# Down weights fetched a block ahead, TensorE in written order and a layer norm in pairs, in a fused forward and backward kernel

## Chip, cores, metric

One core of a Trainium2 chip. The metric is device time in microseconds (us) of one execution; a profile of one execution of each kernel is read beside it. Lower is better. A verdict of faster or slower needs 2%.

## The reference, cut to what matters

The function adds three terms and returns its value with the gradients of nine inputs:

```python
xn = _layernorm(x, axis=-1)                              # x: 2048 x 1024, bf16
return x + conv_branch(xn, k, v, shift_k, ssm_k, ssm_D) + mlp(xn, W_gate, W_up, W_down)

def mlp(x, W_gate, W_up, W_down):                        # 1024 -> 3584 -> 1024
    gate = x @ W_gate;  up = x @ W_up
    gate = gate * (gate > 0)
    return (gate * up) @ W_down
# conv_branch: short shift convolution of k, times v, a long convolution (FFT), times xn
```

The kernel computes the MLP and its gradients with 8064 products of 128x128 by 128x512. The convolution branch, eight groups of 128 channels, is interleaved with them.

## The kernel before

Rows are cut into 16 tiles of 128, hidden columns into 7 blocks of 512. The first phase, `hidden`, runs 14 times (two halves of the rows by 7 columns; I call each a block, 0 to 13). In a block, for pairs of row tiles: a gate product, an up product and a down product (`ps_g`, `ps_u`, `ps_h`; each 8 matrix instructions, 1.73 us). `wg`, `wu` and `wdT` are the block's weights, each of four pieces of 256 KB. A slot set is room for one such weight; there are four, three in use and one spare. A tile of the normalised rows is flipped (transposed) on TensorE (`pst_x`), and VectorE copies it to `xnT`, which the gate and up products read; `goT`, the transposed gradient of the output, comes by DMA transposes.

```python
LN_CHUNKS = (1, 1, 1, 1, 2, 2, 4, 4)        # tiles of the layer norm that are handled together

def gemm8(self, ps, xT, w):
    for kt in range(self.DT):
        self.pri.pin(self.nc.tensor.matmul(ps[:], ...))     # pin: only once the branch runs

# hidden(), one block; sp counts pairs of row tiles
def load_gate(): nw[0] = self.col_block(Wg, nb, "wg", spare)      # at the block's start
def load_up():   nw[1] = self.col_block(Wu, nb, "wu", su)         # after its last up product
def load_down(): nw[2] = self.row_block_T(Wd, nb, "wdT", sg)      # after its last gate product:
                                                                  # four DMA transposes
...
w, sets, spare = tuple(nw), (spare, su, sg), sd
```

All these transfers are issued from one engine, SyncE, in a fixed order: a transfer that waits for something holds up all behind it. The branch runs on a clock of its own: each product counts 1.73 us of "product time", and a step of the branch is written between two products when that clock has passed its turn.

```python
A_START = 55_000                 # ns of product time: the branch's first inputs are asked for
SLOT = 1780                      # ns between steps of the branch, 72 to a group
def steps(self):
    self.shift_rows()            # a small table: TensorE, ScalarE (sk_t), stored to sk_d
    nx = self.loads_1(0)         # hn, gt, xt (xt reads xn_d, the normalised rows), sD
    self.loads_2(nx)             # kp, vt, skb
    yield 16000                  # then the groups begin
    ...
```

## Time and profile before

| | kernel before |
|---|---|
| median of the runs beside the changed kernel | 1953.41 us (1952.6 to 1957.48, 4 runs) |
| span of the profiled run | 1950.2 us |
| first gate product of block 1 | 67.28 us |
| first product after `hidden` (`ps_d`) | 704.07 us |
| TensorE waits for `wu`, `xnT`, `Y` | 10.3, 8.4, 3.2 us |

The two instants cut the span in three: the start, where the layer norm feeds TensorE; blocks 1 to 13; the rest. The prediction below shows the views and how they are read.

### The profile page before, as it was taken

How to read it: one execution, taken by the hardware profiler on the slowest of the kernel's cores; microseconds unless marked ns; L12 is line 12 of the kernel's file. 1: busy time of each engine (PE TensorE's matmuls, PEld its weight loads, DVE VectorE, ACT ScalarE, POOL GpSimd, SP SyncE). 2: the span in 40 equal slices, each digit the busy share in tenths (PEclk: the TensorE clock that was granted, in tenths of full speed). 3: DMA queues.
4: the chain of work that ended last, by engine and by line, in shares of the span. 5: the costliest groups of instructions: out<-in, count | busy, mean ns of one | idle time of the engine just before them, and what ended most of it. 6: DMA issues, size and time to landing. Idle time of an engine off the chain costs nothing.

```text
span 1950.2 us, 35936 instructions
## 1 busy us (share of the span) xinstructions
PE 1896.9 (97%) x15295; PEld 882.9 (45%) x15526; DVE 908.1 (47%) x1358; ACT 628.6 (32%) x861; POOL 15.5 (1%) x38
## 2 busy tenths in 40 slices
PE   8999899999999999999999999999999999999998
PEld 3444444444444444444444444444444444444443
DVE  5777677777676673443443443510222222222222
ACT  5664354354445344344345345321000000000000
POOL 1100000000000000000000000000000000000000
PEclk9999999999999999999999999999999999999999
DMA  9985676974774884464744543376999854554551
GB/s 253 242 193 143 164 185 165 220 195 131 178 179 131 199 231 129 112 175 126 204 128 134 141 125 106 106 192 214 234 254 248 206 132 122 122 121 122 121 124 35
DMA packets 615985, 319.08 MB, mean 164 GB/s; under 512 B 450952, under 2 KB 585104, under 8 KB 615824
## 3 DMA queue, kind: packets, MB, share of 16 engines
q1 hardware_dynamic: 605328, 295.79, 61.4%
q10 hardware_dynamic: 9216, 16.78, 2.8%
q0 software_dynamic: 1280, 4.20, 0.6%
q8 instruction: 121, 1.98, 0.4%
q14 instruction: 40, 0.33, 0.1%
HBM read 141.56 MB, written 95.44 MB: 122 GB/s over the span
## 4 chain that ended last, share of the span: by engine, by line
PE 65%; issue 2%; DMA 0%; DVE 0%; ACT 0%; SPq 0%
PE ps_w L1006 19%; PE ps_x L1188 19%; PE ps_o L1154 10%; PE ps_d L1006 8%; PE ps L72 4%; PE ps_d L1019 1%; PE ps_h L795 1%; PE ps_u L795 1%; PE ps_g L795 1%; PE ps_w L1019 0%; DMA wu<-in_B_W_up_dram 0%; DMA xn_nat<-xn_d 0%; PE pst L304 0%; ACT K L76 0%; DVE flp L315 0%
## 5 line engine op out<-in xcount | busy, mean ns | idle before, releaser
L1006 PE MATMUL ps_w<-ugs,xn_nat 128*128 128x512 bf16 x1674 | 377.1, 379 | 5.0 <-issue 3.2
L795 PEld LDWEIGHTS <-xnT 128*128 128x128 bf16 x1792 | 170.9, 98 | 230.5 <-issue 20.6
L1006 PEld LDWEIGHTS <-xn_nat 128*128 128x128 bf16 x1728 | 165.0, 98 | 199.4 <-issue 5.5
L795 PE MATMUL ps_u<-wu,xnT 128*128 128x512 bf16 x865 | 205.7, 382 | 12.9 <-DMA wu<-in_B_W_up_dram 10.3
L795 PE MATMUL ps_g<-wg,xnT 128*128 128x512 bf16 x864 | 206.3, 384 | 10.9 <-DVE xnT L824 8.4
L795 PE MATMUL ps_h<-wdT,goT 128*128 128x512 bf16 x872 | 202.4, 379 | 2.6 <-issue 1.4
L1201 ACT ACTIVATE w<-xn,m 128x512 f32<-128x512 bf16 x32 | 24.3, 806 | 559.5 <-issue 317.2
L1188 PE MATMUL ps_x<-wgT,ggT 128*128 128x512 bf16 x879 | 197.6, 379 | 0.9
L1188 PE MATMUL ps_x<-wuT,guT 128*128 128x512 bf16 x877 | 197.3, 379 | 0.9
L1154 PE MATMUL ps_o<-wd,hT 128*128 128x512 bf16 x878 | 192.6, 379 | 0.9
L1006 PE MATMUL ps_d<-g_nat,hs 128*128 128x512 bf16 x740 | 167.5, 379 | 3.1 <-issue 2.4
L1154 PEld LDWEIGHTS <-hT 128*128 128x128 bf16 x896 | 87.7, 98 | 105.7
L1188 PEld LDWEIGHTS <-ggT 128*128 128x128 bf16 x896 | 87.7, 98 | 105.7
L1188 PEld LDWEIGHTS <-guT 128*128 128x128 bf16 x896 | 87.7, 98 | 105.7
L899 DVE SCALAR_TENSOR_TENSOR ru<-ru,ps_u 128x512 bf16<-128x512 bf16 x112 | 76.7, 685 | 125.6 <-issue 53.3
L315 DVE STREAM_TRANSPOSE flp<-C 128x1024 f32<-128x1024 f32 x48 | 90.5, 1931 | 93.7 <-ACT C L76 93.7
L795 PEld LDWEIGHTS <-goT 128*128 128x128 bf16 x896 | 85.6, 98 | 104.0 <-issue 4.3
L1190 DVE CUSTOM_DVE_ANT_0 gx<-ps_x,gy 128x512 f32<-128x512 f32 x32 | 22.1, 691 | 216.6 <-PE ps_x L1188 202.5
L76 ACT CAST C<-ps 128x1024 bf16<-128x1024 f32 x96 | 92.5, 1015 | 91.8 <-PE ps L72 91.2
L926 ACT CAST gh<-ps_h 128x512 bf16<-128x512 f32 x112 | 65.3, 584 | 160.2 <-PE ps_h L795 143.5
L315 DVE STREAM_TRANSPOSE flp<-B 128x1024 f32<-128x1024 f32 x48 | 90.6, 1938 | 49.5 <-ACT B L76 49.5
L76 ACT CAST B<-ps 128x1024 bf16<-128x1024 f32 x96 | 94.1, 1016 | 58.8 <-PE ps L72 54.2
(169 smaller groups left out, 1484.1 us busy)
## 6 DMA issues: line engine op xcount, KB each, us to landing
ug_d<-ru SPq DMA_DIRECT2D x112, 256.0 KB, 4.9
ugs<-ug_d SPq DMA_DIRECT2D x112, 256.0 KB, 4.8
wg<-in_B_W_gate_dram SPq DMA_DIRECT2D x56, 256.0 KB, 4.8
wu<-in_B_W_up_dram SPq DMA_DIRECT2D x56, 256.0 KB, 4.9
h_d<-ht SPq DMA_DIRECT2D x112, 128.0 KB, 2.2
hs<-h_d SPq DMA_DIRECT2D x56, 256.0 KB, 4.7
out_dram<-wi SPq DMA_DIRECT2D x56, 256.0 KB, 2.2
gt<-in_grad_out_dram SPq DMA_DIRECT2D x32, 256.0 KB, 5.3
```

The lines of the kernel that those rows point to most:

```text
L72: self.pri.pin(self.nc.tensor.matmul(out, lhsT=lhsT, rhs=rhs, start=start, stop=stop))
L76: self.pri.pin(self.nc.scalar.copy(out=out, in_=in_))
L315: self.pri.pin(self.nc.vector.transpose(out=df[:, c0:c0 + 32, :], in_=sf[:, c0:c0 + 32, :]))
L795: self.pri.pin(self.nc.tensor.matmul(ps[:], lhsT=xT[:, kt * P:(kt + 1) * P], rhs=w(kt), start=(kt == 0), stop=(kt == self.DT - 1)))
L899: self.pri.pin(nc.vector.scalar_tensor_tensor(out=ru[s][:, 1, :], in0=ru[s][:, 0, :], scalar=0.0, in1=ps[:], op0=ALU.is_gt, op1=ALU.mult))
L926: self.pri.pin(nc.scalar.copy(out=gh[:], in_=ps[:]))
L1006: self.pri.pin(self.nc.tensor.matmul(ps[:], lhsT=lhsT(st), rhs=rhs(st), start=(st == 0), stop=(st == self.ST - 1)))
L1019: self.pri.pin(self.nc.tensor.matmul(ps[i][:], lhsT=lhsT(i, st), rhs=rhs(i, st), start=(st == 0), stop=(st == self.ST - 1)))
L1154: nc.tensor.matmul(ps[:], lhsT=hT[:, kt, :], rhs=self.wd[:, kt, oc], start=(kt == 0), stop=(kt == self.FT - 1))
L1188: nc.tensor.matmul(ps[:], lhsT=T[:, kt, :], rhs=W[:, kt, oc], start=(i == 0), stop=(i == n - 1))
L1190: V.tensor_tensor_reduce(out=gx[:, oc], in0=ps[:], in1=gy[:, oc], scale=1.0, scalar=0.0, op0=ALU.add, op1=ALU.add, accum_out=m[:, ob:ob + 1])
L1201: nc.scalar.activation(out=w[:, oc], in_=xn[:, oc], func=ACT.Identity, scale=m[:, 5:6], bias=m[:, 4:5])
```

## The change

Its intent: take the waits away in which TensorE stands for `wu`, for flipped tiles `xnT` and for the branch's product `Y`. Cut to its core:

```diff
-    LN_CHUNKS = (1, 1, 1, 1, 2, 2, 4, 4)
+    LN_CHUNKS = (1, 1, 1, 1, 2, 2, 2, 2, 2, 2)
@@ gemm8, flip_xn, warm: TensorE in written order from the start
-            self.pri.pin(self.nc.tensor.matmul(...))
+            self.pri.pin(self.nc.tensor.matmul(...), always=True)
+            if mid is not None and kt == 3:
+                mid()                                # a flip in the middle of an up product
@@ weights of the next block
-                    nw[0] = self.col_block(Wg, nb, "wg", spare)
+                    nw[0] = self.col_block(Wg, nb, "wg", sg)
-                    nw[2] = self.row_block_T(Wd, nb, "wdT", sg)
+                    nw[2].append(self.row_piece_T(Wd, nb, "wdT", spare, q))
@@ gate_up: wg after the last gate product, wu after the last up product
+                if end:
+                    load_gate()
...
                 if not ahead:
-                    if sp == 0:
-                        load_gate()
                     yield from gate_up(sp)
+                    load_down(sp // 2)
-            w, sets, spare = tuple(nw), (spare, su, sg), sd
+            w, sets, spare = tuple(nw), (sg, su, spare), sd
@@ block 0, first two pairs: gate, flip, up, gate, up (with a flip in it) instead of
@@ flip, gate, flip, gate, up, up; the norm's last two pairs and the branch's tables in block 1
+                if n == 1 and sp < 4:
+                    chunk()
+                    if sp == 2: ... tables()
@@ the branch
-    SLOT = 1780
+    SLOT = 1760
-        yield 16000
+        yield 11000
-A_START = 55_000
+A_START = 66_000
@@ slots(): one step of the complex product before the two flips instead of after
+        yield None, qy
         flg = self.flip(...)
         yield None, flg
         yield None, flg
-        yield None, qy
```

## The prediction

> **What bounds the kernel now.** I read the page's busy times first.
> ```profile
> span 1950.2 us, 35936 instructions
> ...
> PE 1896.9 (97%) x15295; PEld 882.9 (45%) x15526; DVE 908.1 (47%) x1358; ACT 628.6 (32%) x861; POOL 15.5 (1%) x38
> ```
> TensorE is busy for 1896.9 of 1950.2 us, and the change neither adds nor removes one of its products. It can only win the 53.3 us in which TensorE is idle, and time in which it runs at a lower clock. The timeline fixes 7.9 us of the idle time at the end (last product over at 1942.3) and 1.5 us before the first dummy product; the change touches neither. What is left is in the waits of TensorE, by instruction and releaser (total, times, longest):
> ```profile
> PE ps_u L795 <- DMA wu<-in_B_W_up_dram: 10.3, 9, 4.5
> PE ps_g L795 <- DVE xnT L824: 8.4, 6, 3.6
> PE ps L72 <- DVE Y L80: 3.2, 3, 1.7
> ```
> The third row is the convolution branch, the first two the MLP's first phase (`hidden`, until about 705 us). The next view is TensorE in order of time over the first 75 us (start, length, idle time before it in brackets):
> ```profile
> 18.64 0.61 PE L822 MATMUL pst_x<-ident,ln_x 128*128 128x128 bf16 x8
> 21.45 3.58 PE L795 MATMUL ps_g<-wg,xnT 128*128 128x512 bf16 x8 [2.21 <-DVE xnT L824]
> ...
> 40.20 3.62 PE L795 MATMUL ps_u<-wu,xnT 128*128 128x512 bf16 x16
> ...
> 51.77 5.31 PE L795 MATMUL ps_g<-wg,xnT 128*128 128x512 bf16 x16 [3.60 <-DVE xnT L824]
> ```
> Sixteen products take 3.62 us, but 5.31 after a wait of 3.60 us; eight take 1.90 elsewhere and 3.58 after 2.21 us of waiting. A long wait thus costs 1.7 us more in clock. Why the wait at 51.77 is so long is in VectorE and ScalarE around it:
> ```profile
> 48.42 0.17 DVE L746 TENSOR_SCALAR ln_b<-ln_s 128x4 bf16<-128x4 f32 x1 [3.35 <-ACT ln_j L732]
> ...
> 50.42 0.69 DVE L927 TENSOR_TENSOR ru<-ru,gh 128x1024 bf16<-128x1024 bf16 x1
> 51.02 1.29 DVE L824 COPY xnT<-pst_x 128x1024 bf16<-128x1024 bf16 x2
> ```
> TensorE had flipped tiles 6 and 7 by 46.4, but their copies stand in VectorE's queue behind the layer norm of four later tiles, whose four row sums ScalarE finishes at 48.4. Last, the queue of transfers around the longest wait for `wu`, and TensorE there:
> ```profile
> 201.16 5.31 SPq L803 DMA_TRANSPOSE wdT<-in_B_W_down_dram  x4
> 206.56 2.74 SPq L88 DMA_DIRECT2D kp<-in_A_k_dram  x4
> ...
> 213.92 1.97 SPq L788 DMA_DIRECT2D wu<-in_B_W_up_dram  x4
> ```
> ```profile
> 211.68 1.90 PE L795 MATMUL ps_g<-wg,xnT 128*128 128x512 bf16 x7
> 218.13 3.59 PE L795 MATMUL ps_u<-wu,xnT 128*128 128x512 bf16 x8 [4.55 <-DMA wu<-in_B_W_up_dram]
> ```
> `wu` has one slot set, so it can be asked for only when the last up product of a block is over. Four transposes of `wdT` and the branch's next inputs (6.7 us of issuing) stand in the queue before it. In blocks without the branch's inputs the same waits are 0.7 to 1.5 us, ended by the transposes alone.
>
> **What the Trainium skill says.** "TensorE: Matmul & The Clock Gate", Part 1: The HAM clock gate: after an idle window of about 3.4 us the array runs at half rate until about 3.4 us of activity have passed. Half of 3.4 is 1.7, and the three dips here (at 21.45, 51.77, 218.13) cost 1.68, 1.69 and 1.69 us; the first came after only 2.21 us of idling, so the limit isn't sharp here. The same page, Architectural detail: VectorE and ScalarE are strict first-in-first-out; the copies at 51.02 agree. "DMA: Bandwidth & Descriptors", Anatomy of one DMA: a DMA's semaphore wait happens on the issuing sequencer. This agrees: the queue waited 142 us in all (100 to 800 us) for `ht`, with later loads behind it. "Advanced Engine Details and Errata", X-Bar Transpose (TRN2): transposes are as fast as plain transfers. The landing agrees (median 3.4 us against 4.9 for `wu`); but a transpose holds the issuing queue for a median of 1.25 us, a piece of `wu` for 0.42.
>
> **The change, part by part.**
>
> 1. *Order of the weights.* The four transposes leave the place ahead of `wu`: one goes after each pair of rows, into the set that the block before freed. In exchange `wg` loses its second set and is asked for after the block's last gate product. Until its use come two up and two down products, 4 x 1.73 = 6.9 us and up to 2 us of branch work. Four pieces take 2.0 to 2.5 us to issue and land 4.9 us after issue; TensorE eats a piece each 0.43 us. So the first piece has about 2 us in hand and the last about 0.5 (an estimate). `wu` has the same 6.9 us, now with a free queue: in three block changes where the transposes happened to be over early (wu issued at 455.98, 505.74, about 604) it waited for nothing. Gain: 10.3 + 1.7 of clock = 12.0, less 1 left over: 11 us.
>
> 2. *The branch's start and pace.* 55 to 66, then 16 to 11, with 2 after both: the branch's groups start at 79 instead of 73 us of product time. A group is 72 slots, so the eight end at 79 + 576 x 1.76 = 1092.8 instead of 1098.3: nothing for the end. But I placed the loads of `kp`, `vt`, `skb` (slot 50 of a group) in the blocks of 24 x 1.73 = 41.5 us. Before: 73 + 50 x 1.78 = 162.0, that is 37.4 us into a block, between the last gate product (34.6) and the last up product (38.1): the 4.55 us wait. The next is at 41.0. After: 167.0, 0.9 into a block, then 3.1, 5.2, 7.4; none falls into 34.6 to 41.5, where `wg` and `wu` are now asked for. I take this into the 11.
>
> 3. *One half-step of the complex product ahead of the two flips.* At 483.26 the last `Y` step ran behind two flips of 1.9 us, and TensorE began at 483.97. It now goes before them: 2.7 of 3.2 us.
>
> 4. *The first products.* Between the first gate product (10.31) and the end of the gate pair 6, 7 (57.0) lie 18 products of 1.73 and eight flips of 0.55 us: 35.5 of 46.7 us. So 11 us can be lost at most. Traced order makes gate 0, flip 1, up 0, gate 1, half of up 1, flip 2, the rest: each copy (0.69 us) now lies beside at least 0.9 us of products. That takes out 0.8 + 2.2 + 0.8 of waits and 1.7 of clock. Pairs shorten what stands before the copies of tiles 6 and 7 from four row sums (4.4 us) to two (2.3), and from four subtractions (1.68) to two (0.88): about 3 of the 3.6 us and the clock's 1.7. But the norm's own chain sets a floor: tile 2 was normalised at 16.8, 3 at 20.1, 6 and 7 at 39.8, and the fixed order would want them at 17.0, 20.2 and 39.4; I give 1 to 3 us back. Gain: 3.8 + 1.7 + 3 + 1.7 = 10.2, less 2.2: 8 us.
>
> Against it: the branch's first inputs (15 us of issuing, from 83.5 in the profile) now begin 24.5 us into block 1 and so may stand before its `wg` at 34.6; the tables also come a quarter-block later. I put 2.5 us on this.
>
> Sum: 11 + 2.7 + 8 - 2.5 = 19.2; 1952.85 - 19.2 = 1933.7, so **1934 us**, 1.0% less.
>
> **Rivals.** *`wg` takes `wu`'s place as the wait.* For it: one slot set, 0.5 us in hand for the last piece, and stores in the queue ahead. Against: the three block changes without a wait. 13 changes at 0.7 us would eat 9: 1943. *The fixed order stalls TensorE at the start*, as no other product may pass a late tile. For it: the norm's times in 4. Against: at 18 to 27 the scheduler's own order waited as well. The start would give nothing: 1942. *VectorE becomes the bound of the branch with the slot at 1.76.* Against: it is busy for 32 to 39 of each 50 us there; worth a few us at most. *Everything comes off*: all 12 + 3.2 + 11 would be 1926.5.
>
> **Range and chances.** 1925 to 1944: the two first rivals at one end, all gains and a few small issue gaps at the other. Faster by over 2% would need 1913.8, that is 39 us; the idle time that can be had (53.3 - 9.4 - about 5 of dummy and first tile) with 5 of clock comes to 44, of which the change addresses 26. 2%. Slower by over 2%: 1%.
>
> **What would show it.** Right: waits for `wu` under 2 us in all; none for `Y` above 0.5; no wait of over 2 us before a gate product in the first 60 us; block 1's first gate product near 59 instead of 67.28; the same busy time of TensorE after the start. Wrong: a row of waits of gate products for `wg`, above all near 100 us; `pst_x` waiting for `ln_x`; or the saved time coming back as waits of the branch on VectorE.

## The result, and the profile after

The changed kernel took 1940.03 us (median; 1939.31 to 1943.27, 4 runs, none over 1.5% above the fastest), the kernel before 1953.41 beside it. A ratio is the mean time of one kernel's fast runs over the mean of the other's in the same rounds, so not quite the ratio of the medians; here it is 0.9931, 95% interval 0.9913 to 0.9948: 0.7% less. Predicted: 1934, 1925 to 1944. The measured gain, 13.4 us, is 70% of the predicted 19.2.

The page after, to be held against the first two lines that the prediction shows:

```profile
span 1938.3 us, 35924 instructions
...
PE 1891.5 (98%) x15294; PEld 881.5 (45%) x15526; DVE 910.2 (47%) x1378; ACT 630.3 (33%) x863; POOL 15.3 (1%) x38
```

The span is 11.9 us shorter, with TensorE's instructions unchanged. The waits of TensorE after (total, times, longest):

```profile
PE ps_g L795 <- DMA wg<-in_B_W_gate_dram: 9.3, 3, 7.3
PE ps_g L795 <- DVE xnT L827: 3.9, 3, 2.9
...
PE pst_x L824 <- DVE ln_x L776: 1.8, 2, 1.6
...
PE ps L72 <- DVE flp L315: 1.5, 3, 0.8
```

The 10.3 us for `wu` and the 3.2 for `Y` are gone. In their place gate products wait 9.3 us for `wg`, 7.3 of it at once. The waits for `xnT` have halved, and a flip (`pst_x`) waits for a normalised tile.

TensorE in the first 62 us, as in the prediction's third fence:

```profile
22.18 0.62 PE L824 MATMUL pst_x<-ident,ln_x 128*128 128x128 bf16 x8 [1.63 <-DVE ln_x L776]
...
27.39 1.90 PE L795 MATMUL ps_g<-wg,xnT 128*128 128x512 bf16 x8 [2.87 <-DVE xnT L827]
...
47.70 3.63 PE L795 MATMUL ps_g<-wg,xnT 128*128 128x512 bf16 x16 [0.20 <-DVE xnT L827]
...
61.52 3.62 PE L795 MATMUL ps_g<-wg,xnT 128*128 128x512 bf16 x16
```

The gate pair of tiles 6 and 7 begins at 47.70 instead of 51.77, after 0.20 us of waiting instead of 3.60, and takes 3.63 instead of 5.31. But tile 3's flip (22.18) and the gate product behind it (27.39) wait 4.5 us.

The 7.3 us wait, on TensorE:

```profile
106.07 0.59 PE L72 MATMUL ps<-hT,RH 128*128 128x512 bf16 x2
113.96 3.59 PE L795 MATMUL ps_g<-wg,xnT 128*128 128x512 bf16 x8 [7.30 <-DMA wg<-in_B_W_gate_dram]
```

This is the first gate product of block 2; at 3.59 instead of 1.90 us it pays the clock's 1.7 too. What stood in the transfer queue before `wg` (start, time of issuing, transfer):

```profile
88.97 0.34 SPq L96 DMA_DIRECT2D sk_d<-sk_t  x1
...
90.31 1.42 SPq L88 DMA_DIRECT2D gt<-in_grad_out_dram  x2
98.12 1.31 SPq L88 DMA_DIRECT2D xt<-xn_d  x2
...
106.24 1.58 SPq L88 DMA_DIRECT2D skb<-sk_d  x1
...
109.74 2.22 SPq L788 DMA_DIRECT2D wg<-in_B_W_gate_dram  x4
```

And what the queue itself waited for between 80 and 112 us:

```profile
SPq L88 <- DMA xn_d<-ln_x: 6.1, 2, 5.6
SPq L96 <- ACT sk_t L76: 4.6, 1, 4.6
```

The slots of `wg` were free from about 96 us (the last gate product of block 1). It was asked for at 109.74, behind all of the branch's first inputs. In these, `xt` waited for the last normalised rows, which the norm in pairs delivers from block 1 (last store issued at 91.94; before, from 72.14).

By thirds of the span: block 1 begins 5.8 us earlier (67.28 to 61.52), the blocks 1 to 13 take 5.0 us less (636.8 to 631.8), the rest 1.1 us less. At both instants the branch stands at the same step, so the thirds can be compared.

### The profile page after: what moved, and what is told of

It is laid out like the page before. It is cut to its first block, busy times and chain, and to the rows that moved or that the text cites. A ratio compares the mean times of both kernels' runs of the same rounds, so it can differ in the third digit from the quotient of the medians.

```text
span 1938.3 us, 35924 instructions
## 1 busy us (share of the span) xinstructions
PE 1891.5 (98%) x15294; PEld 881.5 (45%) x15526; DVE 910.2 (47%) x1378; ACT 630.3 (33%) x863; POOL 15.3 (1%) x38
## 4 chain that ended last, share of the span: by engine, by line
PE 66%; issue 2%; DMA 0%; DVE 0%; ACT 0%
PE ps_w L1032 19%; PE ps_x L1214 19%; PE ps_o L1180 10%; PE ps_d L1032 8%; PE ps L72 4%; PE ps_h L795 1%; PE ps_u L795 1%; PE ps_d L1045 1%; PE ps_g L795 1%; PE ps_w L1045 1%; DMA ugs<-ug_d 0%; PE pst L304 0%; DMA xn_nat<-xn_d 0%; DVE flp L315 0%; DVE o L1230 0%
## 5 line engine op out<-in xcount | busy, mean ns | idle before, releaser
L1130 ACT CAST wi<-ps_w 128x512 bf16<-128x512 f32 x108 | 63.7, 590 | 154.7 <-PE ps_w L1032 150.0
```

What stands on the lines that cost most here:

```text
L1130: self.pri.pin(nc.scalar.copy(out=wo[0][:, d, :], in_=ps[:]))
```

## The experiments

My theory after the result: the 7.3 us come from the transfer queue, which stands at `xt` until the norm's last rows are stored. Rivals: the volume of the branch's inputs, wherever they stand; and the one slot set of `wg`, which can only be refilled after the last gate product. At the start, I took the two waits left for queue order on ScalarE and VectorE, against the norm's own chain as the floor.

### 1. `xt` behind the other first inputs

```diff
-        self.load_time(xt, self.xn_d, cg)          # third of the first inputs
+        if gi: self.load_time(xt, self.xn_d, cg)
...
         self.loads_2(nx)
+        self.load_time(nx["xt"], ...)              # first group: last
```

> Changed kernel, but for the first group the two loads of xt (which read xn_d) go behind the other first inputs of the branch instead of third. Queue theory (the transfer queue stands at xt from 91.7 to 98.1 us waiting for the last stores of xn_d, and everything behind it, wg of block 2 included, is late by that): the other inputs fill the 6.4 us, wg is asked for 6 to 7 us earlier, its 7.3 us wait falls to 0 to 2 us and the 1.7 us of clock goes too; 1932 us (1930 to 1935). Volume theory (the branch's inputs take the DMA engines, so wg lands late wherever it stands): as many bytes in the same stretch, the wait stays at 5 us or more; 1938 to 1941. One-set theory (wg can only be asked for after the last gate product, that alone is the wait): stays at 7; 1940.

Measured: 1938.4 us, ratio 0.9926 (0.9912 to 0.9941). The queue no longer waits for `xn_d`, but `wg` is asked for at 108.44 instead of 109.74 and TensorE still waits 5.23 us for it there. The issuing of the inputs, from 89.35 to 104.7, has merely lost its gap, and part of the gap was filled by slower issuing (the four pieces of `kp` took 5.04 us instead of 3.60, a store behind the inputs 2.14 instead of 0.36):

```profile
112.27 2.68 PE L797 MATMUL ps_g<-wg,xnT 128*128 128x512 bf16 x6 [5.23 <-DMA wg<-in_B_W_gate_dram]
```

So the wait for `xt` is 2.1 of the 7.3 us. My queue theory in its first form falls; volume and one-set both stand.

### 2. The branch 14 us later

```diff
-A_START = 66_000
+A_START = 80_000
```

> Changed kernel with the branch started 14 us later (80 instead of 66 us of product time), so that its first inputs are asked for after wg and wu of block 2. Queue and volume theory: no wait of gate products for wg at the second block change, 9 us less; but the third group's first inputs then come 30.5 us into block 11 and may cost 1 to 2 us: 1932 (1930 to 1936). One-set theory: the wait stays, 1940. If later placing costs the branch's end anything, TensorE would show waits after 1290 us; I expect none.

Measured: 1931.56 us, ratio 0.9898 (0.9879 to 0.9918). No product waits for `wg` anywhere. The queue:

```profile
94.45 2.13 SPq L788 DMA_DIRECT2D wg<-in_B_W_gate_dram  x4
...
105.36 0.55 SPq L96 DMA_DIRECT2D sk_d<-sk_t  x1
```

`wg` goes out as soon as its slots are free, and the branch's inputs follow behind `wu`. `wg` still has one slot set, and at all 13 block changes nothing waits for it: the one-set theory falls. What counts is that the branch's inputs do not stand between the last gate product and the next block. This run cannot tell the queue from the volume, as both foresaw it. The landing times can: the one that the trace of the changed kernel has for `wg` at this change is 4.6 us after issue, against a median of 4.3 for all of its `wg`. So `wg` was issued late and did not land late; volume can have acted only by slower issuing. In time, the intervals of this run and of the changed kernel still touch (0.9879 to 0.9918, 0.9913 to 0.9948), so it is the waits that show the cause. The 2.0 us of waits for `wg` at the change from block 6 to 7 are gone as well, which I had not expected. The branch pays with one wait of 2.58 us for a flip of its own, at 136 us.

### 3. The norm's last two pairs in block 0 again

```diff
-                if n == 1 and sp < 4:
+                if ahead:
                     chunk()
-                    if sp == 2: ... tables()
+                    if sp == 6: ... tables()
```

> Changed kernel with the last two pairs of the layer norm traced in block 0 again instead of block 1 (pairs kept), the tables right after. Queue theory: the last xn_d store is issued near 75 instead of 92 us, xt waits for nothing, the first inputs are all asked for by 98 and wg 8 us earlier; its wait falls from 7.3 to 0 to 1.5: 1931 to 1934, unless the norm's row sums in block 0 hold back down products there (up to 3 us more: then 1936). Volume theory: wait of 5 or more, 1938 to 1941.

Measured: 1943.27 us, ratio 0.9952 (0.9937 to 0.9967): a miss. `xt` now waits for nothing, yet the wait for `wg` is 8.23 us. The tables, traced earlier, go through ScalarE ahead of the copy `sk_t`; its store, which stands in front of the branch's inputs, is issued at 94.74 instead of 88.97 (the queue waited 4.3 us for `sk_t`), all inputs follow later, and `wg` goes out at 112.70. The earlier norm alone does not help: there is more than one thing for the block of inputs to wait for.

### 4. The norm's chunks of four again

```diff
-    LN_CHUNKS = (1, 1, 1, 1, 2, 2, 2, 2, 2, 2)
+    LN_CHUNKS = (1, 1, 1, 1, 2, 2, 4, 4)
```

> Changed kernel with the old chunks of the layer norm (two of four tiles at the end instead of four pairs). If pairs are what took the 3.6 us wait for the copies of tiles 6 and 7 away: it comes back with 2 to 4 us and possibly the clock's 1.7, block 1's first gate product at 64 to 66 instead of 61.5. Queue theory: the last xn_d store moves from 92 to near 80, so the wait for wg at the second block change falls to 0 to 3 us. Net 1934 to 1940. If pairs gave nothing at the start, 1932.

Measured: 1943.28 us, ratio 0.9954 (0.9934 to 0.9975). The gate pair of tiles 6 and 7 waits 2.19 us again and takes 5.32 us; block 1 begins at 66.42 instead of 61.52. Of these 4.9 us, 1.6 are a clock dip after gate 3 that has nothing to do with the chunks (see 5), so pairs are worth about 3.3 us here: 2.0 of wait and 1.7 of clock before tile 6, less 0.4 of small differences. That takes the dip off in full; if without it the wait for the copies had been longer instead, pairs are worth up to 4.9. The wait for `wg` at the second block change is 4.41 us, a miss against 0 to 3: the queue's wait for `xn_d` is gone altogether (last store issued at 71.25, `xt` at 96.07, 0.3 us after `gt`), and over 4 us stay, as in experiment 1.

### 5. Without the fixed order of TensorE

```diff
-        if self.strict or always:
+        if self.strict:
```

> Changed kernel without the fixed TensorE order before the branch begins (gate, up and down products, flips and dummies again ordered by the scheduler); trace order, pairs and weights unchanged. If the fixed order is what won the start (waits before gate products 8.4 to 3.9 us): block 1's first gate product moves from 61.5 back to 64 to 67 us, total 1942 to 1946. If the order in which the products are written, or the pairs, did it: 61 to 62.5, total 1939 to 1942. The wait for wg at the second block change stays at 5 to 9 us either way.

Measured: 1941.3 us, ratio 0.9954 (0.9934 to 0.9973). The two builds turned out to have the same instructions in the same order on all five engines: with the products written in this order, the scheduler would have kept it. So this part of the change does nothing, and this run is a repeat of the changed kernel. As such it shows two things. The ratio of one program differs by 0.2% (0.9931, 0.9954). And gate 3, after the same wait (2.87 and 2.86 us), took 1.90 us in one profile and 3.43 in the other, so whether a wait of this length costs the clock's 1.7 us differs from run to run:

```profile
27.75 3.43 PE L795 MATMUL ps_g<-wg,xnT 128*128 128x512 bf16 x8 [2.86 <-DVE xnT L827]
```

Block 1 began at 64.12 instead of 61.52.

### 6. The norm of tiles 4 and 5 later

```diff
                 yield from first_gate_up(0)
-                chunk()
-                yield from first_gate_up(2)
+                yield from first_gate_up(2, chunk)     # chunk after tile 3's flip
```

> Changed kernel with the layer norm of tiles 4 and 5 traced after the flip of tile 3 instead of before gate 2. My reading of the two waits left at the start (1.63 us of the flip, 2.87 us of gate 3): tile 3's square root stands behind two row sums of tiles 4 and 5 on ScalarE, its copy behind their norm on VectorE. Then both fall, together from 4.5 to 1 us or less, but tiles 4 and 5 then stand behind the norm of 6 and 7, whose input lands only at 31 us: 1 to 4 us of new waits before gates 4 and 5. Block 1's first gate product at 59 to 61.5; total 1937 to 1940. If instead the norm's own chain is the floor, both waits stay and nothing moves: 61.5, 1940.

Measured: 1941.91 us, ratio 0.9957 (0.994 to 0.9974); experiment 5, in the same rounds, is the control with 0.9954. Tile 3's flip now waits 0.79 us instead of 1.63, and gate 3 not at all: it ends at 25.4 instead of 29.3. So those waits were queue order, not the norm's own chain. But the flip of tile 4 waits 5.7 us:

```profile
34.55 1.89 PE L824 MATMUL pst_x<-ident,ln_x 128*128 128x128 bf16 x16 [5.70 <-DVE ln_x L776]
```

ScalarE shows why (the norm's next row sum, of tile 6, holds the queue until its input lands; the square root of tiles 4 and 5 is behind it):

```profile
31.54 1.06 ACT L732 ACTIVATE ln_j<-ln_x 128x1024 bf16<-128x1024 bf16 x1 [4.61 <-DMA ln_x<-in_A_q_dram]
```

I had named this wait, at 1 to 4 us. Block 1 begins at 64.39, a miss against 59 to 61.5.

### 7. The same, with the input of tiles 6 and 7 asked for earlier

```diff
+    load(5)
     goT = [b.load_T(g, i, "goT", 8 + i) for i in range(4)]
-    load(5)
```

> As the run before, and the input of tiles 6 and 7 asked for ahead of the four transposes of goT (its landing near 24 instead of 31 us). Same reading: the new waits before gates 4 and 5 go too; block 1's first gate product at 57 to 58.5, total 1935 to 1937 with the wait for wg at the second block change still there (7 us, perhaps longer by what TensorE arrives earlier: then up to 1939). If the wait for wg absorbs all of the gain, the total is 1940 although block 1 begins earlier.

Measured: 1943.33 us, ratio 0.9963 (0.9947 to 0.9979). The wait before tile 4 falls to 0.98 us. The next one of its kind appears: a down product waits 3.91 us for `ru` (46.04), behind the norm of tiles 8 and 9, whose input is still late. Block 1 begins at 63.26, a miss against 57 to 58.5. In the chain of the norm, each wait removed so far has uncovered the next; experiment 11 asks for more of the inputs earlier.

### 8. Kernel before, with the weights alone

```diff
-                    nw[0] = self.col_block(Wg, nb, "wg", spare)   # at the block's start
+                    nw[0] = self.col_block(Wg, nb, "wg", sg)      # after the last gate product
-                    nw[2] = self.row_block_T(Wd, nb, "wdT", sg)
+                    nw[2].append(self.row_piece_T(Wd, nb, "wdT", spare, q))   # one per pair
```

> Kernel before with only the new order of the weights (wg asked for after the last gate product, then wu; wdT a piece per pair into the freed set). If the transposes ahead of wu were the cause of its waits: the 0.7 to 1.5 us waits at five block changes go (about 5 us), total 1944 to 1948; at the change where the branch's inputs stand in the queue (4.55 us and 1.7 us of clock) a wait of wu of 1 to 5 us stays, since those are still asked for there. If wg takes their place: waits of gate products for wg of over 5 us in total and 1950 or more.

Measured: 1945.12 us, ratio 0.9971 (0.9954 to 0.9988), as expected. Of the nine waits for `wu` one is left, 3.11 us at the change where the branch's inputs stand in the queue; no product waits for `wg`. From block 1 to the end of `hidden` the profile is 5.3 us shorter. It also has two waits that I had not named and did not follow up: 3.3 us for `goT` in block 0, and 1.5 us of an up product for ScalarE's copy `gh` in block 1.

### 9. Kernel before, with the complex-product step alone

The edit is the last hunk of the change.

> Kernel before with only the branch's complex-product step moved ahead of the two flips. If that order made the three waits of TensorE for Y (3.2 us): they fall to 0.5 us or less, total 2.5 to 3.2 us under the kernel before, about 1948 to 1950. If the flips, now later by a slot, are waited for instead: the waits for flp grow from 0.8 to 3 us and the time stays.

Measured: 1949.88 us, ratio 0.9991 (0.9971 to 1.001). The waits for `Y` are gone (3.2 to 0), those for flips unchanged (0.8). The time does not tell it from nothing: the gain is as small as the repeat error of experiment 5, and the longest wait for `wu` happened to be 5.24 instead of 4.55 us. Shown in the waits, not in the time.

### 10. Kernel before, with the branch's start and pace alone

```diff
-        yield 16000
+        yield 11000
-A_START = 55_000
+A_START = 66_000
-    SLOT = 1780
+    SLOT = 1760
```

> Kernel before with only the branch's start (66 and 11 instead of 55 and 16) and pace (1760 instead of 1780). Placement theory (a load of the MLP's weights waits if the branch's inputs stand ahead of it in the queue): the 4.55 us wait for wu at the fourth block change goes (inputs now 0.9 us into a block), and a new wait for wu of 3 to 8 us comes at the second block change, where the first inputs now stand ahead of wdT and wu; total 1949 to 1955. If the waits for wu have nothing to do with the branch's inputs: the 4.55 us wait stays and none comes.

Measured: 1958.8 us, ratio 1.0037 (1.0015 to 1.0059): slower by 7 us, 4 more than I allowed. The 4.55 us wait is gone, and the new one is where the placement theory puts it, at the second block change:

```profile
120.26 1.44 PE L795 MATMUL ps_u<-wu,xnT 128*128 128x512 bf16 x3 [6.21 <-DMA wu<-in_B_W_up_dram]
```

In this kernel the norm is in its old chunks and `wg` has its second slot set. So neither of them is needed for a wait at this change: the place of the branch's first inputs in block 1 brings one there too. It is not quite the same wait, as here `wu` is the one held up, and four transposes (5.8 us of issuing) still stand between the inputs and it.

### 11. The branch later, the norm later, its inputs earlier

Experiments 2 and 6 together, and `load(5)`, `load(6)` ahead of the transposes of `goT`, `load(7)` right behind them.

> Changed kernel with the branch started at 80, the norm of tiles 4 and 5 traced after the flip of tile 3, and the inputs of the norm's pairs 5, 6 and 7 (tiles 6 to 11) asked for ahead of or between the transposes of goT. If what is left at the start is only that each pair of the norm stands at the head of VectorE's and ScalarE's queues until its input lands behind the transposes: no wait over 1.2 us in the first 70 us, block 1's first gate product at 57 to 58.5, and no wait for wg: total 1924 to 1928. If the order of the norm itself is the floor: a wait of 2 to 4 us appears before a down product or a flip again and the total is 1928 to 1932. If asking early delays goT or wdT: waits of down products for goT.

Measured: 1932.04 us, ratio 0.9903 (0.9888 to 0.9918), no better than experiment 2. The start is as hoped: tiles 6 and 7 begin at 44.58 (46.78 in experiment 2). Then `wg` (2.5 us), `wu` (1.1) and `goT` (1.5) are waited for. In block 0 the transfer queue is never empty: `wg` could have gone out at about 48 and went at 54.62, behind four transposes of `wdT` and one of `goT`.

### 12. The same, with block 1's `wdT` behind `wg` and `wu`

```diff
-                        if sp == 0:
-                            for q in range(4): load_down(q)
                 if ahead and sp + 4 < HS:
                     yield from gate_up(sp + 4)
+                    if sp == 2: ...
+                        for q in range(4): load_down(q)
```

> As the combined run before (branch started at 80, norm of tiles 4 and 5 later, inputs of the norm earlier), but block 1's four pieces of wdT are asked for after wg and wu instead of in the middle of block 0. That run gained the start (gate pair 6, 7 at 44.6 us against 46.8 with the later start alone) and lost it again in waits for wg and wu (3.6 us) and goT (1.5), which I put down to the transfer queue being full with transposes until 54.6 us. If so: wg is asked for near 49 and waits for nothing, at most 1 us of waiting for wdT before block 1's first down product; total 1926 to 1929. If what holds wg back is the volume of block 0's transfers rather than their order: wg or wdT waits for 2 to 4 us as before; 1931 to 1933.

Measured: 1928.87 us (1927.45 to 1929.68), ratio 0.9886 (0.9865 to 0.9907), the fastest of all, 1.1% under the kernel before. `wg` goes out at 47.92 and costs 0.5 us of waiting, `wdT` none. Block 1 begins here:

```profile
58.12 3.62 PE L795 MATMUL ps_g<-wg,xnT 128*128 128x512 bf16 x16
```

Its interval lies below that of the changed kernel (0.9913 to 0.9948), though from other rounds; it overlaps that of experiment 2, so the later start is the certain part and the better start of about 2.5 us rests on the profile.

## Why the prediction was right, and where it was not

Time, range and class held, and most steps did. Some of the size is luck: by the repeat in experiment 5 (0.9954) the gain is about 9 us, not 13. Of the signs of being wrong that the prediction named, two came: gate products wait for `wg` (one long wait from 106.6 us, where a row of waits was named, and two short ones later), and `pst_x` waits for `ln_x`; and of the signs of being right, "no wait of over 2 us before a gate product in the first 60 us" failed (2.87). The terms, as the prediction has them:

| step | predicted | measured | from |
|---|---|---|---|
| 1. weights | 11 | 10.0 | waits for `wu` 10.3 and clock 1.7 gone; 2.0 of new waits for `wg` at the change from block 6 to 7 |
| 3. complex product | 2.7 | 2.5 | waits for `Y` 3.2 gone, for flips 0.7 more |
| 4. start | 8 | 5.8 | block 1 at 61.52 instead of 67.28 |
| "Against it" | -2.5 | -9.0 | wait for `wg` 7.3 and clock 1.7 |
| sum | 19.2 | 9.3 | |
| time | 19.2 | 13.4 (medians), 11.9 (profiles) | |

2.6 us of the profile's gain are in no row: 1.1 lie after `hidden`, the others are spread over small gaps, and 0.2% is the repeat error.

- **Step 1 held**, mechanism and size: the waits for `wu` go with the new order of the weights alone (experiment 8, whose edit moves `wdT` and `wg` together). The rival that `wg` takes the place of `wu` because of its one slot set is refuted by experiments 2 and 8, in which no product waits for `wg`. The two small waits for `wg` in the change from block 6 to 7 are the 0.5 us in hand, overdrawn: two transposes of `goT` stood before it.
- **Step 2 held in both halves.** The placement of the later inputs, worked out from 72 slots and blocks of 41.5 us, took away the 4.55 us wait (experiment 10). It was not carried to the first inputs as strictly.
- **The step that failed is the term "Against it"**: "the branch's first inputs ... may stand before its `wg` at 34.6; ... I put 2.5 us on this." The wait came at that place for that reason (experiments 2 and 10), but measured 7.3 us and 1.7 of clock. The term was too small even by the prediction's own numbers: inputs from 24.5 us into the block, 15 us long, end at 39.5, 4.9 us behind the place of `wg`, which had about 2 us in hand; with the clock's 1.7 that is some 4.6 us (an estimate), and I put 2.5. Beyond that I left out that the inputs can wait themselves: for the table `sk_t` (4.6 us) and for the norm's last rows (6.1 us), which the pairs had moved into block 1. `wg` went out 13.6 us behind its place (61.52 + 34.6 = 96.1): the 4.9 us, 3.0 because the store of `sk_d` began 27.45 us into the block, 3.9 because the inputs took 18.9 us from there to the last one, and 1.9 for two stores behind them. Taking away the wait for the norm's rows alone leaves 5.23 us of waiting (experiment 1) or 4.41 (experiment 4); no run takes away the wait for `sk_t` alone, so its share is argued, not shown.
- **Step 4 was too high by 2.2 us.** Its order part was put at 3.3 us (5.5 less 2.2 for the norm's floor) and came to 0.6 up to the first down product (31.47 to 30.86), although that stretch's clock dip of 1.7 us had gone: tile 3's copy came to stand behind the norm of tiles 4 and 5 as tiles 6 and 7's had before. Its pairs part was put at 4.7 (3, and 1.7 of clock) and is about 5.2 between the two single profiles, 3.3 to 4.9 by experiment 4. The fixed order is no part of it (experiment 5). How much of the clock's 1.7 us a run has differs from run to run, and so the 5.8 itself is uncertain by a us or two: with the old start, block 1 begins at 65.61 to 68.32 in four profiles (kernel before, experiments 8, 9 and 10), with the new one at 60.60 to 64.12 in four (changed kernel, experiments 1, 2 and 5).
- **Two slips in the prediction's sums** change nothing in it. Seven flips, not eight, lie between 10.31 and 57.0, which makes 35.0 of 46.7 us and 11.7 that can be lost; and all gains together give 1926.65, not 1926.5.

What stays open: why experiment 2 also loses the waits at the change from block 6 to 7, and how the 2.5 us of experiment 12 over experiment 2 look in time with more runs. For the first, the queue gives a hint: in the changed kernel two stores of the branch's `gv` come shortly before (345.62), the two transposes of `goT` begin 0.2 us after the last gate product and take 4.31 us; in experiment 2 no such store stands there, and they begin 1.3 us before that product is over and take 2.67.

## What to carry to other kernels

When several streams of work share one in-order transfer queue, draw up for each weight load the stretch between the freeing of its slots and its use, and keep every other batch of loads, the first one above all, out of it; count a batch with the waits of its own members, not with its issuing alone. Work that you delay to smooth one place (the norm in pairs) may be what such a batch waits for. And compare two builds' instruction order before timing them: a "fixed order" may be the order you already had.

## What the Trainium skill lacked or had wrong

- "TensorE: Matmul & The Clock Gate", Part 1: The HAM clock gate, ties the half clock to an idle window of about 3.4 us. Shorter waits brought it here: 2.21 us (kernel before, 1.68 us lost) and 2.19 us (experiment 4, 1.7 lost). Not every such wait did: 2.05 and 2.19 us at the place of the first lost nothing (experiments 8 and 10). The page's free-running window agrees with the runs: after 2.87 and 2.86 us in the same program, one run lost nothing and the other 1.5 us.
- "Advanced Engine Details and Errata", X-Bar Transpose (TRN2), calls transposes as fast as plain transfers. That held for the landing (median 3.4 us against 4.9 for `wu` in the kernel before, 5.5 against 5.8 in the changed one); no page has a time for issuing a transpose of this size, which decided here: one of 256 KB holds the issuing queue for 1.25 us (median of `wdT` in the kernel before; 2.6 each for the first four of the changed kernel, 10.44 us together), a plain piece of `wu` for 0.42.
- No page says how far the issuing of one and the same load varies: the four loads of `kp` took 3.60 us of the queue in the changed kernel and 5.04 in experiment 1, where no pause came before them. That it slows because more is in flight is my reading; no run shows it.
